# Two spectral and two attention layers on one core: constant matmuls and another order around the start of attention, another end of the layer

## The chip, the cores and the metric

The kernel runs on one core of a Trainium2 chip. A core has a matrix engine (TensorE, PE in the profile), a vector engine (VectorE, DVE), a scalar engine (ScalarE, ACT), a general one (GpSimd, POOL) and SyncE (SP), which only issues transfers. PE writes to PSUM, which the others read. The metric is the device time of one execution in microseconds (us); less is better. Before the change it is 1662.77 us, the median of three runs.

## The reference, cut to what matters

```python
def _layernorm(x):                       # over the last axis, eps 1e-5, no weights
    ...
def _A_ref(x, w_r, w_i):                 # spectral layer, x is 1 x 2048 x 512 bf16
    X = rfft2(x) * (w_r + 1j * w_i)
    return irfft2(X, s=(2048, 512)).astype(bf16)
def _B_ref(x, wq, wk, wv, wo):           # attention, 32 heads of 16, one k and one v for all heads
    q = (x @ wq).reshape(B, S, 32, 16).transpose(0, 2, 1, 3)
    k, v = x @ wk, x @ wv
    p = softmax(einsum("bhqd,bkd->bhqk", q, k) * 16 ** -0.5)
    o = einsum("bhqk,bkd->bhqd", p, v)
    return o.transpose(0, 2, 1, 3).reshape(B, S, 512) @ wo
x = x + A(layernorm(x));  x = x + B(layernorm(x))
x = x + A(layernorm(x));  x = x + B(layernorm(x))
```

## The kernel before

The 2048 tokens are split by their number modulo 4 into four blocks t, and each block into four tiles r of 128 tokens; `x_sb[:, r, t, :]` is the running sum and `xn_sb` its layernorm, both bf16 in SBUF. The layers run in the order A, B, A, B.

*Spectral layer* (`spectral_layer`). The transform over tokens begins with matmuls of `xn_sb` with tables (`over_s_sums`, L192), copied by ACT into `G` (`over_s_out`, L197); `over_s(3)` does the last block inside the layer, the blocks before it are done at the end of the attention layer ahead of it. Transforms over the other axis, the product with the weights and the way back follow. The end is `back_s(t)`: for each tile four matmuls (L391); even r add x by a matmul with the identity (L394) and are copied by ACT (L395), odd r are added by DVE (L397), and then `layernorm_group` takes the statistics of a pair of tiles (DVE, L125/L126), a square root (ACT, L128) and writes xn (L134 ACT, L136 POOL).

*What attention needs first* (`attention_inputs`). `block(t)` transposes xn into `xT` by eight and eight matmuls with the identity (L469), the first half copied by ACT (L472), the second by DVE (L474); four K matmuls (L478), copied into `KT` by ACT (L479); `kmax`, a maximum over KT by DVE (L480); 16 V matmuls (L485), whose result goes to `vaug` in four scaled copies, two by ACT (L490), two by DVE (L492). These share two PSUM banks ("mm"). `block(t - 1)` follows `back_s(t)`; `block(3)` comes last, and then `close`: an exponential of one column (L501), which makes ACT load its table, the bound of KT (L502, L503), and half of KT's rows rewritten (L505).

*Attention* (`attention_layer`) runs over 32 groups g (8 sets of 4 heads for each of 4 query blocks) in 514 steps n. A step has up to three score tiles of 128 keys by 512 queries for ACT (`act_step`: matmuls L583 into the three banks of `sc`, two such tiles in turn; one exponential L683 over all three) and one for DVE (`dve_step`: L583 into the bank `dv`, then L707 and L713, an exponential in integer arithmetic, whose error four scales of `vaug` even out). The matmuls with the values (`pv_step`, L695) come `LAG = 2` steps later and add up in one bank, `pv`. At the change of group the bank is copied by DVE (L598), its sums are inverted by way of DRAM, POOL normalises (L633, L639), and the queries of a later group are projected (L455 to L461). `chain()` fixes on each of PE, ACT, DVE and POOL the order in which the program was written.

*The layer's end* (L796 on). The output projection (`outproj`, L661) of tile k; `finish` adds x and stores to `x_sb`, either by ACT where a matmul with the identity has added x (L667), or by DVE (L669). `statistics` and `normal(t)` are the next layernorm (L756 to L776); `sequence(first)` does the `over_s_sums` of three units (one unit is a t and a quarter of the columns), `sequence_out` their copies to `G`. The last group's part is added to block four's tiles (k = 12 to 15) once POOL has normalised it (L633 `od`, then `woO` in L661). In the last layer `nxt` is None: no statistics, no sequences; `finish` also stores the output (L914).

Of the kernel before, what the change touches and what calls it, by code (L numbers as in the profile page):

```python
# [9 lines left out]
ACT = mybir.ActivationFunctionType  # L10
ALU = mybir.AluOpType
P = 128
# [6 lines left out]
NC = 4  # L19
# [77 lines left out]
def build_tables(nc, const):  # L97
# [5 lines left out]
    mhalf = const.tile([P, 1], F32, name="mhalf")  # L103
    nc.vector.memset(mhalf, -0.5)
    c["mhalf"] = mhalf
# [13 lines left out]
def layernorm_group(nc, lnpool, tabs, tiles):  # L119
# [3 lines left out]
    for i, (x_ap, _, _) in enumerate(tiles):  # L123
        stats = lnpool.tile([P, 6], F32, tag="ln_stats", bufs=4)
        nc.vector.bn_stats(stats, x_ap)  # L125
        nc.vector.bn_aggr(mv[:, i, :], stats)  # L126
# [74 lines left out]
def spectral_layer(nc, tc, tabs, shared, lnpool, x_sb, xn_sb, WT, WX, aw, nxt, loads):  # L201
# [5 lines left out]
    with (tc.tile_pool(name="workA", bufs=1) as work,  # L207
# [179 lines left out]
        def back_s(t):  # L387
            for r in range(R):
                ps = psum.tile([P, 512], F32, tag="pa")
                for k, (c, part) in enumerate(((0, 0), (0, 1), (1, 0), (1, 1))):  # L390
                    nc.tensor.matmul(ps, lhsT=IT[:, t, part, c, r * P:(r + 1) * P], rhs=U[:, t, part, c, :],  # L391
                                     start=(k == 0), stop=(k == 3 and r % 2 == 1))
                if r % 2 == 0:
                    nc.tensor.matmul(ps, lhsT=tabs["ident"], rhs=x_sb[:, r, t, :], start=False, stop=True)  # L394
                    nc.scalar.copy(out=x_sb[:, r, t, :], in_=ps)  # L395
                else:
                    v.tensor_tensor(out=x_sb[:, r, t, :], in0=ps, in1=x_sb[:, r, t, :], op=ALU.add)  # L397
                    layernorm_group(nc, lnpool, tabs, [(x_sb[:, q, t, :], xn_sb[:, q, t, :], (g, nc.scalar)[q % 2])
# [38 lines left out]
        prep["block"](T - 1, psum_b)  # L437
        prep["close"](xn_sb[:, R - 1, T - 1, 0:1])
# [3 lines left out]
def attention_inputs(nc, tabs, shared, xn_sb, aw):  # L442
# [21 lines left out]
    def block(t, psum):  # L464
        for half in range(2):
# [5 lines left out]
            if half == 0:  # L471
                nc.scalar.copy(out=dst, in_=ps)  # L472
            else:
# [6 lines left out]
        nc.vector.tensor_reduce(out=kmax[:, t:t + 1], in_=KT[:, ks], axis=mybir.AxisListType.X,  # L480
                                op=ALU.max, apply_absolute_value=True)
        psv = psum.tile([P, 4, DH], F32, tag="mm")
        for i in range(4):
            for c in range(NC):
                nc.tensor.matmul(psv[:, i, :], lhsT=xT[t][:, c, i, :], rhs=wv_sb[:, c, :],  # L485
                                 start=(c == 0), stop=(c == NC - 1))
        for j in range(4):
# [11 lines left out]
    def close(xn_last):  # L499
        dmyo = shared.tile([P, 1], F32, tag="dmyo", bufs=1)  # L500
        nc.scalar.activation(out=dmyo, in_=xn_last, func=ACT.Exp)  # L501
        nc.vector.tensor_reduce(out=kb[:, 0:1], in_=kmax, axis=mybir.AxisListType.X, op=ALU.max)  # L502
        nc.vector.tensor_scalar(out=kb[:, 1:2], in0=kb[:, 0:1], scalar1=tabs["KAB"][:, 1:2], scalar2=None, op0=ALU.mult)  # L503
        for a, b in ((0, 512), (512, S)):
            nc.vector.tensor_scalar(out=KT[:, a:b], in0=KT[:, a:b], scalar1=tabs["KAB"][:, 0:1], scalar2=kb[:, 1:2],  # L505
                                    op0=ALU.mult, op1=ALU.add)

# [469 lines left out]
```

## Time and profile before

| | us |
|---|---|
| runs | 1660.22, 1662.77, 1667.63 |
| median | 1662.77 |
| the profiled execution's own time | 1662.98 |
| its span, first to last instruction | 1661.2 |

| engine | busy us | share of the span | instructions |
|---|---|---|---|
| PE | 1404.5 | 85% | 12606 |
| DVE | 1549.5 | 93% | 2796 |
| ACT | 1506.4 | 91% | 1250 |
| POOL | 164.6 | 10% | 278 |

The mean granted TensorE clock is 0.971 of full speed. The page gives busy times, the span cut into 40 slices with the busy share of each in tenths, and the groups of instructions; a trace behind it answers for any stretch. A row of the timeline reads: start, duration, engine, line, operation, output <- inputs, partitions x elements and type, count, and in brackets the idle time before it with what ended it. For a matmul, 128*128 is rows * columns of the array, 32*128 a strip of 32 rows. PE's ends are modelled, so overlapping matmuls can show more busy time than they block.

### The profile page before, as it was taken

Reading aid. Unit: us, or ns where it says so; the run is one execution under the profiler, and the core shown is the slowest. Engines: PE = TensorE matmul, PEld = TensorE weight load, DVE = VectorE, ACT = ScalarE, POOL = GpSimd, SP = SyncE. Lnnn points to the kernel's source line nnn. Section 1 sums busy time; section 2 is a strip of 40 time slices with the busy share of each in tenths; the row PEclk is TensorE's granted clock in tenths of the full one; section 3 lists DMA queues with packets and bytes.
Section 4 is the critical chain, followed back from the end, with each engine's and each line's share of the span. In section 5 each row is a group of like instructions: output and inputs, shape, how many; then the busy total and the mean of one; then the engine's idle time right before and its main releaser. Section 6 shows DMA issues by size and latency. Waiting matters only on the chain.

```text
span 1661.2 us, 32022 instructions
## 1 busy us (share of the span) xinstructions
PE 1404.5 (85%) x12606; PEld 453.6 (27%) x12688; DVE 1549.5 (93%) x2796; ACT 1506.4 (91%) x1250; POOL 164.6 (10%) x278
## 2 busy tenths in 40 slices
PE   6778888888888888888888888888888888888887
PEld 3331222222222222222233222222222222222222
DVE  6977999999999999999778689999999999999996
ACT  5368999999999999999854689999999999999994
POOL 3210000000000000000112000000000000000002
PEclk9887999999999999999999689999999999999999
DMA  8000000000000010000020000000000000000002
GB/s 287 5 1 8 17 16 12 15 16 17 17 16 17 17 28 16 17 17 29 23 70 0 1 8 16 17 17 17 17 17 17 17 14 13 17 16 17 16 16 66
DMA packets 46535, 40.76 MB, mean 25 GB/s; under 512 B 30832, under 2 KB 34416, under 8 KB 46000
## 3 DMA queue, kind: packets, MB, share of 16 engines
q1 hardware_dynamic: 45712, 36.88, 7.6%
q8 instruction: 99, 1.62, 0.4%
q0 software_dynamic: 672, 1.84, 0.3%
q14 instruction: 52, 0.43, 0.1%
HBM read 33.57 MB, written 3.15 MB: 22 GB/s over the span
## 4 chain that ended last, share of the span: by engine, by line
DVE 39%; ACT 24%; PE 17%; issue 17%; DMA 1%; POOL 1%; DVEq 0%; SPq 0%; POOLq 0%; ACTq 0%
ACT e L683 23%; DVE t_new L707 15%; DVE s_new L713 12%; PE pv_new L695 6%; PE dv L583 3%; DVE o L598 2%; PE sc L583 2%; DVE qt L460 2%; PE fd L268 2%; DVE qt L461 2%; DVE stats L125 1%; PE ps L391 1%; PE ps L379 1%; DVE den L606 1%; PE ps L192 1%
## 5 line engine op out<-in xcount | busy, mean ns | idle before, releaser
L683 ACT ACTIVATE e<-sc 128x1536 bf16<-128x1536 f32 (+1 forms) x1028 | 1387.0, 1524 | 17.9 <-PE sc L583 17.5
L707 DVE TENSOR_SCALAR t_new<-dv 128x512 int16<-128x512 f32 x1016 | 693.9, 683 | 40.0 <-PE sc L583 21.1
L713 DVE TENSOR_SCALAR s_new<-t_new 128x2048 int16<-128x2048 int16 x1016 | 696.0, 686 | 0.0
L583 PE MATMUL dv<-qt,KT 32*128 32x512 bf16 x1016 | 389.9, 384 | 124.0 <-DVE t_new L707 116.3
L583 PE MATMUL sc<-qt,KT 32*128 32x512 bf16 x3080 | 423.7, 390 | 35.9 <-ACT e L683 3.2
L695 PE MATMUL pv_new<-s_new,vaug 128*32 128x512 bf16 x4064 | 413.3, 394 | 27.3 <-DVE qt L460 27.3
L695 PE MATMUL pv_new<-e,vaug 128*32 128x512 bf16 x3080 | 410.4, 387 | 0.4 <-ACT e L683 0.4
L583 PEld LDWEIGHTS <-KT 32*128 32x128 bf16 x4096 | 201.0, 91 | 731.2 <-issue 715.3
L695 PEld LDWEIGHTS <-vaug 128*32 128x32 bf16 x7144 | 135.7, 94 | 278.2 <-issue 264.7
L639 POOL TENSOR_TENSOR ot_new<-o,rb 128x176 bf16<-128x176 f32 (+1 forms) x96 | 56.4, 590 | 709.9 <-DVE s_new L713 653.1
L639 POOL TENSOR_TENSOR od<-o,rb 128x176 bf16<-128x176 f32 (+1 forms) x90 | 49.4, 549 | 597.5 <-DVE s_new L713 597.5
L455 PE MATMUL ps<-xT,wq_sb 128*128 128x512 bf16 x196 | 62.3, 378 | 13.9 <-DVE o L598 10.7
L379 PE MATMUL ps<-tab_PS,st 128*128 128x512 bf16 x126 | 34.1, 433 | 17.1 <-DVE st L327 13.9
L385 ACT CAST U<-ps 128x512 bf16<-128x512 f32 x24 | 14.1, 586 | 35.4 <-PE ps L379 35.4
L268 PE MATMUL fd<-X,tab_DT 128*128 128x512 bf16 x186 | 41.9, 379 | 3.1 <-DVE X L242 2.8
L460 DVE CAST qt<-ps 128x512 bf16<-128x512 f32 x64 | 44.2, 690 | 0.0
L598 DVE COPY o<-pv_new 128x512 f32<-128x512 f32 x64 | 43.8, 684 | 0.0
L274 ACT CAST xn_sb<-fd 128x512 bf16<-128x512 f32 x32 | 18.8, 586 | 26.9 <-PE fd L268 26.2
L125 DVE BATCH_NORM_STATS2 stats<-x_sb 128x6 f32<-128x512 bf16 x48 | 31.7, 676 | 7.1 <-ACT x_sb L395 3.7
L455 PEld LDWEIGHTS <-wq_sb 128*128 128x128 bf16 x256 | 24.5, 96 | 39.2 <-issue 15.2
L391 PE MATMUL ps<-U,IT 128*128 128x512 bf16 x122 | 32.2, 379 | 0.4
L192 PE MATMUL ps<-FT,xn_sb 128*128 128x512 bf16 x79 | 20.0, 406 | 14.4 <-ACT xn_sb L134 10.9
(134 smaller groups left out, 568.7 us busy)
## 6 DMA issues: line engine op xcount, KB each, us to landing
rb<-d SPq DMA_DIRECT2D x256, 64.0 KB
FT<-const_FT SPq DMA_DIRECT2D x8, 512.0 KB
IT<-const_IT SPq DMA_DIRECT2D x8, 512.0 KB
x_sb<-in_A_x_dram SPq DMA_DIRECT2D x4, 512.0 KB
ot_new<-od SPq DMA_DIRECT2D x120, 16.0 KB
out_dram<-x_sb POOLq DMA_DIRECT2D x14, 128.0 KB, 2.1
tab_DT<-const_DT SPq DMA_DIRECT2D x1, 1280.0 KB
wr_raw<-in_A_w_r_dram SPq DMA_DIRECT2D x1, 1028.0 KB
```

What stands on the lines that cost most here:

```text
L268: nc.tensor.matmul(pss[i], lhsT=DT[:, b, w, 128 * fb:128 * fb + 128], rhs=X[:, b, part, c, :, :].rearrange("p k j -> p (k j)"), start=star ...
L379: nc.tensor.matmul(ps, lhsT=st[c][:, t, vec, q, fb, :], rhs=PS[:, fb, w, :], start=(k == 0), stop=(k == 3))
L391: nc.tensor.matmul(ps, lhsT=IT[:, t, part, c, r * P:(r + 1) * P], rhs=U[:, t, part, c, :], start=(k == 0), stop=(k == 3 and r % 2 == 1))
L455: nc.tensor.matmul(ps, lhsT=wq_sb[:, c, hg, :], rhs=xTq[qb][:, c, :], start=(c == 0), stop=(c == NC - 1))
L460: nc.vector.tensor_copy(out=qt, in_=ps)
L583: nc.tensor.matmul(dst, lhsT=KT[hs, kc * P:(kc + 1) * P], rhs=QT[g][hs, :], start=True, stop=True)
L598: nc.vector.tensor_copy(out=o, in_=pv.pop(g))
L639: pace(nc.gpsimd.tensor_tensor(out=dst[:, a:b], in0=o[:, a:b], in1=rb[:, a:b], op=ALU.mult))
L683: nc.scalar.activation(out=e[:, 0:na, :], in_=sc[:, 0:na, :], func=ACT.Exp, scale=SCALE)
L695: nc.tensor.matmul(pv[g][32 * h:32 * h + 32, :], lhsT=vaug[:, max(j, 0), kc, :], rhs=rhs, start=(first_pv[(g, h)] == u), stop=(last_pv[(g, ...
L707: nc.vector.tensor_scalar(out=tb[(g, kc // 4)][:, kc % 4, :], in0=dv, scalar1=T_MUL, scalar2=T_ADD, op0=ALU.mult, op1=ALU.add)
L713: image[0] = nc.vector.tensor_scalar(out=s_new, in0=tb[(g, b)], scalar1=0.5, scalar2=16384.0 + PH_OFF[j], op0=ALU.mult, op1=ALU.add)
```

## The change

1. The constant `mhalf` goes; a 128 x 128 bf16 tile `zero` is set by POOL.
2. In `back_s`, the very last tile (r = 3, t = 3) adds x by the identity matmul and is copied by ACT, its statistics are read from PSUM, and the xn of r = 2 is written by DVE instead of POOL.
3. `block(t)` takes `kmax` from PSUM instead of from KT. In the built program it still stands behind the KT copy, and the bank is held until it is done.
4. `block(3)` gets 24 matmuls of 128*128x512 whose result (`idle`, in a bank of the other pool) is used by nothing: six with xn (in the built order one stands ahead of block 2's K matmuls and five behind its V matmuls), six with the first half of xT behind ACT's copy of it, ahead of K, and twelve with xT behind the V matmuls.
5. `close` is called inside `block(3)`, before the copies to `vaug`, and its one-column exponential reads xT instead of xn.
6. At step 1 of each attention layer six matmuls of `zero` with KT go into the bank of pv[0], which the first of them starts; group 0's matmuls then only add. At steps 2 to 5 two more each.
7. The layer's end: three of block four's tiles (all but the second) take x by the identity matmul and are finished by ACT. Their last part and `finish` come right behind the first sequence, ahead of `normal(2)`. The sequences are 3, 1, 3, 3 and 2 units long, the single ones in the banks of dv and pv, the copies to G bank by bank.

In all PE has 38 matmuls more in each attention layer with its lead-in.

```diff
-    mhalf = const.tile([P, 1], F32, name="mhalf")
-    nc.vector.memset(mhalf, -0.5)
-    c["mhalf"] = mhalf
+    zero = const.tile([P, P], BF, name="zero")
+    nc.gpsimd.memset(zero, 0.0)
+    c["zero"] = zero
...
-def layernorm_group(nc, lnpool, tabs, tiles):
+def layernorm_group(nc, lnpool, tabs, tiles, sums=None):
 
     n = len(tiles)
     mv = lnpool.tile([P, n, 2], F32, tag=f"ln_mv{n}", bufs=4)
     for i, (x_ap, _, _) in enumerate(tiles):
         stats = lnpool.tile([P, 6], F32, tag="ln_stats", bufs=4)
-        nc.vector.bn_stats(stats, x_ap)
+        nc.vector.bn_stats(stats, sums[i] if sums else x_ap)
         nc.vector.bn_aggr(mv[:, i, :], stats)
...
-                if r % 2 == 0:
-                    nc.tensor.matmul(ps, lhsT=tabs["ident"], rhs=x_sb[:, r, t, :], start=False, stop=True)
+                                     start=(k == 0), stop=(k == 3 and r % 2 == 1), skip_group_check=True)
+                if r % 2 == 0 or (r, t) == (R - 1, T - 1):
+                    nc.tensor.matmul(ps, lhsT=tabs["ident"], rhs=x_sb[:, r, t, :], start=False, stop=True,
+                                     skip_group_check=True)
                     nc.scalar.copy(out=x_sb[:, r, t, :], in_=ps)
                 else:
                     v.tensor_tensor(out=x_sb[:, r, t, :], in0=ps, in1=x_sb[:, r, t, :], op=ALU.add)
+                if (r, t) == (R - 1, T - 1):
+                    layernorm_group(nc, lnpool, tabs, [(x_sb[:, q, t, :], xn_sb[:, q, t, :], (v, nc.scalar)[q % 2])
+                                                       for q in (r - 1, r)], (x_sb[:, r - 1, t, :], ps))
+                elif r % 2 == 1:
                     layernorm_group(nc, lnpool, tabs, [(x_sb[:, q, t, :], xn_sb[:, q, t, :], (g, nc.scalar)[q % 2])
                                                        for q in (r - 1, r)])
 
...
-        prep["block"](T - 1, psum_b)
-        prep["close"](xn_sb[:, R - 1, T - 1, 0:1])
+        prep["block"](T - 1, psum_b, psum)
...
+    def filler(psum, rhs, n):
+
+        ps = psum.tile([P, 512], F32, tag="pa", name="idle")
+        for _ in range(n):
+            nc.tensor.matmul(ps, lhsT=tabs["ident"], rhs=rhs, start=True, stop=True)
+
+    def close(last):
+        dmyo = shared.tile([P, 1], F32, tag="dmyo", bufs=1)
+        nc.scalar.activation(out=dmyo, in_=last, func=ACT.Exp)
+        nc.vector.tensor_reduce(out=kb[:, 0:1], in_=kmax, axis=mybir.AxisListType.X, op=ALU.max)
+        nc.vector.tensor_scalar(out=kb[:, 1:2], in0=kb[:, 0:1], scalar1=tabs["KAB"][:, 1:2], scalar2=None, op0=ALU.mult)
+        for a, b in ((0, 512), (512, S)):
+            nc.vector.tensor_scalar(out=KT[:, a:b], in0=KT[:, a:b], scalar1=tabs["KAB"][:, 0:1], scalar2=kb[:, 1:2],
+                                    op0=ALU.mult, op1=ALU.add)
+
+    def block(t, psum, psum_idle=None):
+        if psum_idle is not None:
+            filler(psum_idle, xn_sb[:, 0, t, :], 6)
         for half in range(2):
             ps = psum.tile([P, 2, NC, P], BF, tag="mm")
             for i in range(2):
...
             dst = xT[t][:, :, 2 * half:2 * half + 2, :].rearrange("d c i p -> d i c p")
             if half == 0:
                 nc.scalar.copy(out=dst, in_=ps)
+                if psum_idle is not None:
+                    filler(psum_idle, xT[t][:, 0:2, 0:2, :], 6)
             else:
                 nc.vector.tensor_copy(out=dst, in_=ps)
         ks = slice(t * 512, (t + 1) * 512)
...
         for c in range(NC):
             nc.tensor.matmul(ps, lhsT=wka[:, c, :], rhs=xTq[t][:, c, :], start=(c == 0), stop=(c == NC - 1))
         nc.scalar.copy(out=KT[:, ks], in_=ps)
-        nc.vector.tensor_reduce(out=kmax[:, t:t + 1], in_=KT[:, ks], axis=mybir.AxisListType.X,
+        nc.vector.tensor_reduce(out=kmax[:, t:t + 1], in_=ps, axis=mybir.AxisListType.X,
                                 op=ALU.max, apply_absolute_value=True)
         psv = psum.tile([P, 4, DH], F32, tag="mm")
         for i in range(4):
             for c in range(NC):
                 nc.tensor.matmul(psv[:, i, :], lhsT=xT[t][:, c, i, :], rhs=wv_sb[:, c, :],
                                  start=(c == 0), stop=(c == NC - 1))
+        if psum_idle is not None:
+            filler(psum_idle, xTq[t][:, 0, :], 12)
+        if t == T - 1:
+            close(xT[t][:, NC - 1, 0:1, 0])
         for j in range(4):
             dst = vaug[:, j, 4 * t:4 * t + 4, 0:DH]
             if j % 2 == 0:
...
                 qproj(g, ps)
                 QT[g] = qevict(ps)
 
-    def close(xn_last):
-        dmyo = shared.tile([P, 1], F32, tag="dmyo", bufs=1)
-        nc.scalar.activation(out=dmyo, in_=xn_last, func=ACT.Exp)
-        nc.vector.tensor_reduce(out=kb[:, 0:1], in_=kmax, axis=mybir.AxisListType.X, op=ALU.max)
-        nc.vector.tensor_scalar(out=kb[:, 1:2], in0=kb[:, 0:1], scalar1=tabs["KAB"][:, 1:2], scalar2=None, op0=ALU.mult)
-        for a, b in ((0, 512), (512, S)):
-            nc.vector.tensor_scalar(out=KT[:, a:b], in0=KT[:, a:b], scalar1=tabs["KAB"][:, 0:1], scalar2=kb[:, 1:2],
-                                    op0=ALU.mult, op1=ALU.add)
-
-    return {"xT": xT, "KT": KT, "QT": QT, "qproj": qproj, "qevict": qevict, "block": block, "close": close}
+    return {"xT": xT, "KT": KT, "QT": QT, "qproj": qproj, "qevict": qevict, "block": block}
 
 
 def attention_layer(nc, tc, tabs, shared, lnpool, x_sb, xn_sb, aw, prep, nxt, store):
...
-                                 start=(first_pv[(g, h)] == u), stop=(last_pv[(g, h)] == u),
+                                 start=(g > 0 and first_pv[(g, h)] == u), stop=(last_pv[(g, h)] == u),
...
+            if n == 1:
+                pv_new = psp.tile([P, 512], F32, tag="pv")
+                pv[0] = pv_new
+                for i in range(6):
+                    nc.tensor.matmul(pv[0], lhsT=tabs["zero"], rhs=KT[:, 0:512], start=(i == 0), stop=False,
+                                     skip_group_check=True)
             if n in qproj_at:
                 ps = psp.tile([P, 512], F32, tag="pv")
                 qproj(qproj_at[n], ps)
                 later(1, lambda g=qproj_at[n], ps=ps: QT.__setitem__(g, qevict(ps)))
             else:
                 pv_step(n)
+            if LAG <= n < LAG + 4:
+                for _ in range(2):
+                    nc.tensor.matmul(pv[0], lhsT=tabs["zero"], rhs=KT[:, 0:512], start=False, stop=False,
+                                     skip_group_check=True)
...
-        def sequence(first):
+        def sequence(first, banks):
             if nxt is None:
                 return None
-            units = [divmod(u, 4) for u in range(first, first + 3)]
-            ps = psc.tile([P, 3, 512], F32, tag="sc", name="seq")
-            for i, (t, b) in enumerate(units):
-                over_s_sums(nc, nxt, xn_sb, t, b, ps[:, i, :])
-            return units, ps
+            units = [divmod(u, 4) for u in range(first, first + len(banks))]
+            for (t, b), ps in zip(units, banks):
+                over_s_sums(nc, nxt, xn_sb, t, b, ps)
+            return units, banks
 
         def sequence_out(arg):
             if nxt is None:
                 return
-            units, ps = arg
-            for i, (t, b) in enumerate(units):
-                over_s_out(nc, nxt, t, b, ps[:, i, :])
+            for (t, b), ps in zip(*arg):
+                over_s_out(nc, nxt, t, b, ps)
+
+        def three():
+            if nxt is None:
+                return []
+            ps = psc.tile([P, 3, 512], F32, tag="sc", name="three")
+            return [ps[:, i, :] for i in range(3)]
 
...
-        ps_a = psc.tile([P, 3, 512], F32, tag="sc", name="tri")
+        ps_a = psc.tile([P, 3, 512], F32, tag="sc", name="three")
+        pf = [ps_a[:, i, :] for i in range(3)]
         ps_b = psp.tile([P, 512], F32, tag="pv")
-        pf = [ps_a[:, 0, :], ps_a[:, 1, :], ps_a[:, 2, :], ps_b]
+        pf.append(ps_b)
         for i in range(4):
-            outproj(12 + i, pf[i], i % 2 == 0)
+            outproj(12 + i, pf[i], i != 1)
         rest()
-        statistics((9, 10, 11))
-        q0 = sequence(0)
+        statistics((9, 10))
+        q0 = sequence(0, three())
         sequence_out(q0)
-        rest = normal(2)
-        rest()
         for i in range(4):
             outproj(12 + i, pf[i], False, last_group=True)
         for i in range(4):
-            finish(12 + i, pf[i], i % 2 == 0)
-        q1 = sequence(3)
+            finish(12 + i, pf[i], i != 1)
+        ps_d = psd.tile([P, 512], F32, tag="dv", name="ps_d") if nxt is not None else None
+        q1 = sequence(3, [ps_d])
+        sequence_out(q1)
+        statistics((11,))
+        rest = normal(2)
+        q2 = sequence(4, three())
+        rest()
         statistics((12, 13, 14, 15))
-        sequence_out(q1)
+        sequence_out(q2)
+        q3 = sequence(7, three())
         rest = normal(3)
         rest()
-        for first in (6, 9):
-            q2 = sequence(first)
-            sequence_out(q2)
+        sequence_out(q3)
+        ps_e = psp.tile([P, 512], F32, tag="pv", name="ps_e") if nxt is not None else None
+        ps_f = psd.tile([P, 512], F32, tag="dv", name="ps_f") if nxt is not None else None
+        q4 = sequence(10, [ps_e, ps_f])
+        sequence_out(q4)
```

More of the change, by code (lines that the diff above doesn't have):

```diff
@@ L391, in back_s @@
                     nc.tensor.matmul(ps, lhsT=IT[:, t, part, c, r * P:(r + 1) * P], rhs=U[:, t, part, c, :],
-                                     start=(k == 0), stop=(k == 3 and r % 2 == 1))
-                if r % 2 == 0:
-                    nc.tensor.matmul(ps, lhsT=tabs["ident"], rhs=x_sb[:, r, t, :], start=False, stop=True)
+                                     start=(k == 0), stop=(k == 3 and r % 2 == 1), skip_group_check=True)
+                if r % 2 == 0 or (r, t) == (R - 1, T - 1):
+                    nc.tensor.matmul(ps, lhsT=tabs["ident"], rhs=x_sb[:, r, t, :], start=False, stop=True,
+                                     skip_group_check=True)
                     nc.scalar.copy(out=x_sb[:, r, t, :], in_=ps)
@@ L462, in qevict @@
         return qt
-    def block(t, psum):
+    def filler(psum, rhs, n):
[13 more added lines that the diff above has]
+            filler(psum_idle, xn_sb[:, 0, t, :], 6)
         for half in range(2):
```

## The prediction

> **What bounds the kernel now.** I read the page's head and slices first, then the busy time by stretches, then the start of each attention layer instruction by instruction. Times are us; the columns of a stretch are its length, the busy time and count of PE, PEld, DVE, ACT and POOL, the granted TensorE clock, the DMA share and GB/s.
>
> ```profile
> span 1661.2 us, 32022 instructions
> ...
> PEclk9887999999999999999999689999999999999999
> 200.00:700.00 500.00, 428.62 (x4157) 131.12 (x4176) 494.76 (x837) 500.00 (x372) 37.87 (x69) 1.00 0.06 17
> ```
>
> In the steady part of attention ACT never idles: 372 exponentials in 500 us, 1.344 us a step, with DVE at 99%. The change touches nothing there. What it can touch are the two dips of PEclk, at slices 3 and 4 and at slices 23 and 24, where attention begins.
>
> ```profile
> 118.50:158.45 39.95, 33.32 (x24) 0.63 0.00 1
> 939.50:978.94 39.44, 33.24 (x24) 0.65 0.00 1
> 117.40:147.50 30.10, 23.84 (x17) 0.50 0.00 1
> ```
>
> These are the exponentials of L683 alone (busy ACT, then clock, DMA share, GB/s). The first 24 steps of each layer take 39.95 and 39.44 us, where 24 x 1.344 = 32.3 would do. From 117.40 to 147.50 the clock is 0.50 from end to end, and in layer two the mean is as low, 0.65. The chain inside one such step:
>
> ```profile
> 130.04 0.60 PE L583 MATMUL dv<-qt,KT 32*128 32x512 bf16 x1
> ...
> 131.00 0.62 PE L695 MATMUL pv_new<-s_new,vaug 128*32 128x512 bf16 x4
> 131.18 1.45 ACT L683 ACTIVATE e<-sc 128x1536 bf16<-128x1536 f32 x1 [0.47 <-PE sc L583]
> ...
> 131.97 0.60 PE L583 MATMUL dv<-qt,KT 32*128 32x512 bf16 x1
> ```
>
> The next scores start 1.93 us after the last (130.04 to 131.97), and ACT idles 0.47 us for its scores each time. So PE at half clock sets the pace here, and nowhere else in attention.
>
> Why the clock falls shows in the stretches between its changes. In layer one it falls at 113.77 and rises at 147.90, ten times 3.413 us later; in layer two it falls at 929.55. Cut backwards from the falls in pieces of that length, the last windows at full clock are the first four rows, and the low stretch (PE alone) is the fifth:
>
> ```profile
> 103.53:106.94 3.41, 2.07 (x21) 1.28 (x19) 3.25 (x12) 3.12 (x7) 0.97 (x2) 1.00 0.00 0
> 106.94:110.35 3.41, 2.03 (x28) 1.31 (x28) 1.58 (x6) 2.35 (x6) 0.90 (x2) 1.00 0.00 0
> 110.35:113.77 3.42, 1.17 (x10) 0.77 (x12) 1.02 (x3) 1.90 (x4) 0.00 (x0) 1.00 0.00 0
> 926.14:929.55 3.41, 1.48 (x21) 0.88 (x21) 1.70 (x7) 2.31 (x5) 1.53 (x2) 1.00 0.00 0
> 113.77:147.90 34.13, 30.88 (x175) 0.50 0.00 1
> ```
>
> The clock held after windows with 2.07 and 2.03 us of PE work and fell after 1.17 and 1.48. Then it did not rise through ten windows in which PE was 90% busy. So busy time alone isn't what lifts it: the work of those windows is narrow (32 rows or 32 columns of the array, the 32*128 and 128*32 above), and where it did rise, PE ran full 128*128 matmuls (the stretches again of PE alone, the last two rows of matmuls one by one):
>
> ```profile
> 885.18:888.59 3.41, 3.41 (x10) 0.50 0.00 0
> 888.59:892.00 3.41, 3.41 (x18) 1.00 0.00 0
> ...
> 884.60 4.30 PE L379 MATMUL ps<-tab_PS,st 128*128 128x512 bf16 x10
> 843.84 5.34 PE L192 MATMUL seq<-FT,xn_sb 128*128 128x512 bf16 x24 [1.27 <-ACT x_sb L667]
> ```
>
> One window of full matmuls, 4.30 / 10 = 0.43 us each at half clock, and the next stands at 1.00; at full clock one costs 5.34 / 24 = 0.22.
>
> **The change part by part.** Per layer it adds 24 full matmuls ahead of the first score (6 with xn, 6 after ACT's xT copy, 12 after the V matmuls) and 14 zero matmuls into pv[0] (6 at step 1, 2 at each of steps 2 to 5), changes two orders and rebuilds the layer's end. Here is the lead-in of layer one that the 24 are laid into, and its counterpart in layer two:
>
> ```profile
> 109.04 0.57 ACT L479 CAST KT<-ps 128x512 bf16<-128x512 f32 x1
> 109.64 0.69 DVE L480 TENSOR_REDUCE kmax<-KT 128x1 f32<-128x512 bf16 x1 [1.35 <-ACT KT L479]
> 109.75 1.28 ACT L501 ACT_TABLE_LOAD   x1
> ...
> 111.25 1.00 ACT L472 COPY xT<-ps 128x1024 bf16<-128x1024 bf16 x1
> 111.76 0.61 PE L469 MATMUL ps<-tab_ident,xn_sb 128*128 128x128 bf16 x8 [1.50 <-DVE vaug L492]
> 113.15 1.32 PE L478 MATMUL ps<-xT,wka 128*128 128x512 bf16 x3 [0.79 <-DVE xT L474]
> 116.38 0.99 DVE L505 TENSOR_SCALAR KT<-KT,tab_KAB,kb 128x512 bf16<-128x512 bf16 x2
> 117.43 0.60 PE L583 MATMUL dv<-qt,KT 32*128 32x512 bf16 x1 [2.54 <-DVE KT L505]
> 118.51 10.18 ACT L683 ACTIVATE e<-sc 128x1536 bf16<-128x1536 f32 x7 [2.31 <-PE sc L583]
> ...
> 929.07 0.57 ACT L479 CAST KT<-ps 128x512 bf16<-128x512 f32 x1
> 938.43 0.60 PE L583 MATMUL dv<-qt,KT 32*128 32x512 bf16 x1 [2.54 <-DVE KT L505]
> ```
>
> *The clock.* With six more full matmuls (1.3 us) the windows ending near 110 and 929.5 come to about 3.3 and 2.8 us; the next holds six more and the K matmuls, the next the twelve, and the one over the first scores the zeros. All lie above the 2.03 that held. If the clock holds to the first steps, these run at 1.344 from the start: 39.95 - 32.3 = 7.6 and 39.44 - 32.3 = 7.1. I leave 0.8 of each standing, since two steps at the first change of group remain long even after the clock is back (exponentials 1.90 apart):
>
> ```profile
> 153.87 1.45 ACT L683 ACTIVATE e<-sc 128x1536 bf16<-128x1536 f32 x1 [0.39 <-PE sc L583]
> 155.77 5.48 ACT L683 ACTIVATE e<-sc 128x1536 bf16<-128x1536 f32 x4 [0.45 <-PE sc L583]
> ```
>
> Gain 6.8 + 6.3 = 13.1; bounds: 14.7 if nothing stays, and 11.5 if 1.6 of each stays. The first score to first exponential, 1.08 at half clock (117.43 to 118.51), halves in its matmul part: -0.45 a layer, -0.9.
>
> [...]
>
> *The lead-in.* From the KT copy of block 2 to the first score it takes 8.4 in layer one and 9.4 in layer two, whose clock fell earlier. kmax now reads PSUM, but comes behind the KT copy still, and its bank comes free only after the reduce: block 3's transposes wait for kmax (end 110.33) instead of for the copy (109.61), +0.6. Against that the table load (1.28) leaves the path of ACT's xT copy, which ran 111.25 to 112.25 behind it; now it can follow the transposes at 110.8. The second eight are then done near 111.5, not 112.37; the six fillers behind ACT's xT copy (111.8) stand ahead of K on PE: 6 x 0.22 = 1.3, to 113.1, where K started at 113.15. K ends at 114.2; the table load at 113.1 is out of the way of the KT copy; kmax, kb and KT follow as before to 117.2. The twelve, 2.6 from 114.8, end at 117.4, beside that DVE chain. So layer one: 0 (+1 if a semaphore comes late on each side, -0.3 if K's own 0.3 at half clock is gained), taken as +0.2; layer two: the same 8.4 instead of 9.4, -0.8. Together -0.6. Were the cover of DVE's chain gone, the twelve would cost their 2.6.
>
> *The zeros.* The six at step 1 (1.3) lie where pv has not begun; two a step add 0.43 to a step in which PE's weight loads show a gap of this size at full clock:
>
> ```profile
> 156.12 0.09 PEld L583 LDWEIGHTS <-KT 32*128 32x128 bf16 x1 [0.42 <-issue]
> ```
>
> Four such gaps of 0.42 take 4 x 0.43 almost whole: 0 to +0.8 a layer, nearer 0; +0.4 for both.
>
> *The spectral layer's end.* The last tile through an ident matmul and an ACT copy, xn by DVE and kmax in another place swap pieces of 0.4 to 0.8 between ACT, DVE and POOL: 0, bounds -0.5 and +0.5 a layer.
>
> *The layer's end* (once, at 835 to 853; the last layer has no spectral work behind it):
>
> ```profile
> 841.83 0.56 ACT L667 CAST x_sb<-tri 128x512 bf16<-128x512 f32 x1
> ...
> 847.75 1.52 ACT L773 ACTIVATE xn_sb<-x_sb,nb,rstd 128x512 bf16<-128x512 bf16 x2 [0.50 <-DVE nb L768]
> 849.17 3.00 ACT L197 CAST G<-seq 128x512 bf16<-128x512 f32 x6
> 852.22 1.02 PE L192 MATMUL ps<-FT,xn_sb 128*128 128x512 bf16 x4 [3.05 <-ACT G L197]
> ```
>
> The finishing copies move ahead of normal(2), so up from 841.83 by about its two ACT passes, 1.5 to 2. But normal(2) and the statistics of tile 11, which stood in front, now stand between them and the last xn passes (847.75 to 849.27): these come at the same time or up to 0.4 later. What is won is at the end: over_s(3) waits for three copies of G (half of the 3.00) from 849.6 instead of six from 849.17, so starts at 851.2 to 851.5 instead of 852.22. -0.75, between -1.2 (the xn passes not later) and +0.3 (two of the single banks waiting a copy each of 0.5).
>
> *The tail.*
>
> ```profile
> 1656.72 0.68 DVE L669 TENSOR_TENSOR x_sb<-ps_b,x_sb 128x512 bf16<-128x512 f32 x1
> 1656.90 0.59 ACT L667 CAST x_sb<-tri 128x512 bf16<-128x512 f32 x1 [0.81 <-DVE x_sb L669]
> ```
>
> The last tile moves from DVE to behind ACT's: done at 1658.1 instead of 1657.40. Its store follows, the other stores overlap: +0.3, between 0 and +0.7.
>
> *Sum.* The profiled run took 1662.98 (span 1661.2 and 1.8 around it), the median is 1662.77; they are one level. 1662.98 - 13.1 - 0.9 - 0.6 + 0.4 + 0 - 0.75 + 0.3 = 1648.3. With all terms at one bound it is 1643.5 or 1655; 1644.5 to 1652 unless they all go one way.
>
> **The rivals.** (a) *The clock falls all the same in the first steps*, because zeros don't count or two a step are too few. The clock held above 2.03 us of work, but steady attention holds it too with 428.62 of 500; against: the start differs from steady work by its first two steps without pv, which the six zeros fill. If so, 13.1 and 0.9 are lost and the 14 zeros at 0.43 lie on PE's path: of 6 us a layer in all, half in steps whose pv work is short: 0 to +3 a layer; 1661 to 1667, say 1663.
>
> (b) *One layer of two, or half of each.* The window's phase is free, and layer two's last K window had 1.48. Where the clock falls before the fillers, twelve in a row at 0.43 (5.2) fill one window and lift it, as ten did at 884.60; the fillers then cost 2 to 3 on the lead-in. 1662.98 less half of 14 plus 0 to 2: 1655 to 1658.
>
> (c) *Slower: the added work runs at half clock throughout.* If 24 fillers don't keep it up, the six ahead of K (2.6 instead of 1.3) push K and all behind it by 1.3; the twelve, 5.2 from 116.2, end at 121.4, 2.7 after KT is ready (117.4 + 1.3); the zeros add 14 x 0.43 = 6 on the PE that sets the pace there. Up to 10 a layer, 1683; it decides once the first score finds the clock at 0.50. Against it: 16 full matmuls (12 added, 4 of K) within the two windows from 108; one window of them lifted the clock at 885.18.
>
> (d) *The layer's end loses.* With q1 and q4 in banks of dv and pv there is more waiting between copies and matmuls; six copies of G take 3.00, so no more than that: +3 on the forecast, 1651.
>
> **How the numbers follow.** The clock held, with or without (d): 0.72 ((d) 0.06 of it). (b): 0.11. (a): 0.09. (c): 0.08. One layer's gain alone, 7, is near 0.5% (8.3 us, about the least that a measurement of this kernel tells from no change). So faster: 0.72 and a small part of (b), 0.74; same: most of (b) and (a), 0.18; slower: (c), 0.08. The likeliest one's range is 1644.5 to 1652; reaching through (b) to the lower end of (a), so as to leave out no more than two in ten, 1643.5 to 1661. Predicted: 1648.3.
>
> **What would show it.** PEclk at 9 in slices 3 and 23; 1.00 in each stretch from 110 to 150 and its counterpart; the first 24 exponentials of a layer within 33 to 34 us; first score 8.4 after block 2's KT copy in both layers; over_s(3)'s matmuls behind the third copy of G, some 0.7 earlier after the last od; the last ACT copy behind the last but one. Wrong if the clock shows 0.50 after the first score for more than one window, if K waits for fillers beyond 113.2, or if ACT still idles for sc at step 10.

## The result, and the profile after

The changed kernel took 1649.27 us, median of five runs (1648.27 to 1655.24), against 1662.77 before (the three runs above and two more, 1660.22 to 1667.63): ratio 0.9921, 95% interval 0.9894 to 0.9948. That is 13.5 us less; 1648.3 was predicted, with 1643.5 to 1661 as the range.

The profiled one of the five is the slowest. From its page:

```profile
span 1653.4 us, 32260 instructions
PEclk9899999999999999999998999999999999999999
```

The dips at slices 3 and 4 and at 23 and 24 are gone; the 8 of slice 2 stands in both kernels, that of slice 22 lies in the spectral layer. What the row can't show, since its 9 stands for 90% or more, is why this execution is slow: a finer cut shows 0.95, not 1.00, nearly everywhere in it; its mean is 0.943, that of the four others 0.992 or 0.993 at spans of 1646.5 to 1647.9. So that a clock of 1.00 is compared with a clock of 1.00, the rows of after come from a second profile of the unchanged changed kernel, run e1 below (1646.76, span 1645.0). The exponentials alone, first 24 steps of each layer (length, busy ACT, clock, DMA share, GB/s):

```profile
117.70:150.44 32.74, 31.92 (x24) 1.00 0.01 2
927.84:960.72 32.88, 32.04 (x24) 1.00 0.01 2
```

39.95 and 39.44 us have become 32.74 and 32.88, where the steady pace would give 32.3, at 1.00 instead of 0.63 and 0.65. The 0.95 execution does nearly the same (32.94 and 33.08); what it loses is elsewhere, the largest part, 3.85 of the 8.4 us by which its span is longer than e1's, between over_s(3) and block 2's KT copy (80.45 us, e1 76.60).

The lead-in of layer one in e1, by the timeline:

```profile
108.74 0.56 ACT L502 CAST KT<-ps 128x512 bf16<-128x512 f32 x1
109.33 0.69 DVE L503 TENSOR_REDUCE kmax<-ps 128x1 f32<-128x512 f32 x1 [0.96 <-ACT KT L502]
110.72 1.01 ACT L493 COPY xT<-ps 128x1024 bf16<-128x1024 bf16 x1 [0.31 <-PE ps L490]
111.75 1.28 ACT L476 ACT_TABLE_LOAD   x1
111.79 1.46 PE L472 MATMUL idle<-xT,tab_ident 128*128 128x512 bf16 x6 [0.44 <-ACT xT L493]
113.08 1.03 PE L501 MATMUL ps<-xT,wka 128*128 128x512 bf16 x3
114.35 2.75 PE L472 MATMUL idle<-xT,tab_ident 128*128 128x512 bf16 x12
116.01 0.99 DVE L480 TENSOR_SCALAR KT<-KT,tab_KAB,kb 128x512 bf16<-128x512 bf16 x2
117.07 0.39 PE L601 MATMUL dv<-qt,KT 32*128 32x512 bf16 x1
117.72 1.45 ACT L701 ACTIVATE e<-sc 128x1536 bf16<-128x1536 f32 x1 [1.88 <-PE sc L601]
```

It reads as it was worked out: xT's copy no longer behind the table load, six constant matmuls in front of K at 0.22 each, K where it was, the twelve (114.35 to 117.10) ending with the DVE chain (117.00), beside it and not behind it.

The stages of both profiles, from the start of one instruction to the start of the next (us; each is a difference of two starts in the trace):

| stage | before | after (e1) | difference |
|---|---|---|---|
| start to KT copy of block 2 | 109.04 | 108.74 | -0.30 |
| KT copy to first score, layer one | 8.39 | 8.33 | -0.06 |
| first score to first exponential | 1.08 | 0.65 | -0.43 |
| 24 steps | 39.94 | 32.72 | -7.22 |
| step 24 to 488 | 625.11 | 625.07 | -0.04 |
| step 488 to the last `od` | 51.23 | 50.71 | -0.52 |
| `od` to over_s(3) | 17.43 | 16.05 | -1.38 |
| over_s(3) to KT copy of block 2 | 76.85 | 76.60 | -0.25 |
| KT copy to first score, layer two | 9.36 | 8.33 | -1.03 |
| first score to first exponential | 1.08 | 0.65 | -0.43 |
| 24 steps | 39.43 | 32.87 | -6.56 |
| step 24 to 488 | 625.10 | 626.23 | +1.13 |
| step 488 to the last `od` | 49.23 | 49.81 | +0.58 |
| `od` to the end | 7.94 | 8.22 | +0.28 |

The differences add up to -16.2, the difference of the spans (1661.2 and 1645.0). That is more than the 13.5 between the medians: e1's profile is of the fastest of its five executions.

The largest loss, step 24 to 488 of layer two, wasn't forecast. 1.2 us more than before stand there in the profiles of every version with the new orders (e5 and e7 to e12 below) and in none of those without them (e2, e3, e4, e6); in e1 eight steps lose 0.12 to 0.25 us each, most of them 64 steps apart. So the orders cost it, whatever the constants and the layer's end do. Why isn't settled.

The layer's end in e1, timeline:

```profile
826.23 1.27 POOL L651 TENSOR_TENSOR od<-o,rb 128x512 bf16<-128x512 f32 x1 [2.77 <-DMA rb<-d]
831.25 0.60 ACT L685 CAST x_sb<-three 128x512 bf16<-128x512 f32 x1
839.26 1.52 ACT L801 ACTIVATE xn_sb<-x_sb,nb,rstd 128x512 bf16<-128x512 bf16 x2 [0.50 <-DVE nb L796]
840.69 1.54 ACT L197 CAST G<-three 128x512 bf16<-128x512 f32 x3
842.28 3.61 PE L192 MATMUL ps<-FT,xn_sb 128*128 128x512 bf16 x16 [2.91 <-ACT G L197]
```

Counted from `od`, the last xn passes start at 13.03 (before: 847.75 - 834.79 = 12.96), the copies of G at 14.46 (before 14.38), and over_s(3) behind the third copy at 16.05 instead of behind the sixth at 17.43.

### The profile page after: what moved, and what is told of

The parts are those of the page before. It is cut to its first block, busy times and chain, and to the rows that moved or that the text cites. A ratio compares the mean times of both kernels' runs of the same rounds, so it can differ in the third digit from the quotient of the medians.

```text
span 1653.4 us, 32260 instructions
## 1 busy us (share of the span) xinstructions
PE 1428.4 (86%) x12768; PEld 461.3 (28%) x12768; DVE 1551.4 (94%) x2793; ACT 1509.0 (91%) x1254; POOL 163.2 (10%) x277
## 4 chain that ended last, share of the span: by engine, by line
ACT 32%; DVE 29%; issue 21%; PE 16%; POOL 1%; DMA 1%; SPq 0%; DVEq 0%; POOLq 0%; ACTq 0%
ACT e L701 31%; DVE t_new L725 11%; DVE s_new L731 9%; PE pv_new L713 4%; PE fd L268 2%; PE dv L601 2%; DVE o L616 2%; DVE qt L464 2%; PE sc L601 2%; DVE qt L465 1%; DVE stats L125 1%; PE tri L679 1%; PE ps L391 1%; PE ps L379 1%; PE ps L192 1%
## 5 line engine op out<-in xcount | busy, mean ns | idle before, releaser
L601 PE MATMUL dv<-qt,KT 32*128 32x512 bf16 x1016 | 384.1, 378 | 108.1 <-DVE t_new L725 106.0
L601 PE MATMUL sc<-qt,KT 32*128 32x512 bf16 x3080 | 409.0, 383 | 33.9 <-ACT e L701 4.3
L459 PE MATMUL ps<-xT,wq_sb 128*128 128x512 bf16 x256 | 67.3, 387 | 11.4 <-DVE o L616 11.4
L379 PE MATMUL ps<-tab_PS,st 128*128 128x512 bf16 x128 | 36.1, 448 | 16.2 <-DVE st L327 12.7
```

The costliest lines, as they stand in the source:

```text
L379: nc.tensor.matmul(ps, lhsT=st[c][:, t, vec, q, fb, :], rhs=PS[:, fb, w, :], start=(k == 0), stop=(k == 3))
L459: nc.tensor.matmul(ps, lhsT=wq_sb[:, c, hg, :], rhs=xTq[qb][:, c, :], start=(c == 0), stop=(c == NC - 1))
L601: nc.tensor.matmul(dst, lhsT=KT[hs, kc * P:(kc + 1) * P], rhs=QT[g][hs, :], start=True, stop=True)
```

## The experiments

All times are medians against runs of the kernel before in the same job (one set of runs on one chip); their medians lay at 1664 to 1666. The ratio on record isn't the quotient of the two medians (e1: 1648.31 / 1664.99 = 0.9900); gains are read from it, with its interval. "Full" matmuls are 128*128 by 512 columns.

**e1: the change again.**

> The changed kernel once more, since the profiled run of it stood at a granted clock of 0.95 from end to end (span 1653.4) while its four other runs have a mean of 0.992 and spans of 1646.5 to 1647.9. Theory (clock gained at the start of attention): median 1648 to 1650; a profile at 1.00 shows the first 24 exponentials of each layer in 32.5 to 33.5 us (39.95 and 39.44 before), first score 8.4 us after block 2's KT copy. Rival (the gain has another source): these 24 steps still take over 36 us.

Measured: 1648.31 (1646.76 to 1653.21), ratio 0.9913 (0.9898 to 0.9929). The rows above are its profile; the theory's numbers hold, the rival's don't.

**e2, e3, e4: the constants alone, and each kind alone.** To the kernel before:

```diff
+        filler(psum_idle, ...)            # e2, e3: 6 with xn, 6 after ACT's xT copy, 12 after V
...
+            if n == 1: six matmuls of zero into pv[0]          # e2, e4
+            if LAG <= n < LAG + 4: two more                    # e2, e4
```

> Before, with the 24 constant matmuls ahead of the first score and the 14 zero matmuls of each layer, every order and the layer's end as before. Theory (clock): 1649 to 1651, 12 to 14 us less than before, PEclk 1.00 from block 3 on in both attention layers. Rival (the new orders and the layer's end bring most): less than 5 us gained.

> Before, with the 24 constant matmuls alone. Theory (the zeros carry the clock over the first two steps, which have no pv): the clock is 1.00 at the first score and falls within two windows, 7 us; nearly nothing gained, 1660 to 1664. Rival (once up, the steps' own work holds it): 1649 to 1651, as with the zeros.

> Before, with the 14 zero matmuls of each layer alone; the first score finds the clock at 0.50. Theory (full matmuls lift the clock where narrow ones don't): the six at step 1, 2.6 us at half clock, and the two a step fill one window, the clock rises near 125 and 946 instead of 147.9 and 967.1: 1654 to 1658. Rival (14 in this spread are too few): the clock stays at 0.50 to 148 and the zeros cost up to 3 us a layer, 1664 to 1669.

Measured: e2 1651.98, ratio 0.9931 (0.9917 to 0.9945); e3 1659.23, 0.9970 (0.9958 to 0.9982); e4 1657.84, 0.9969 (0.9953 to 0.9984). Both kinds together bring 0.69% of e1's 0.87%, either alone 0.30 or 0.31. e2 lies 1 us above what was expected, and its profile isn't at 1.00 all through: the clock falls for one window in layer one, 145.36 to 148.77, at the first change of group, and those 24 steps take 33.87. e3 gained more than the "nearly nothing" of its theory. Windows of 3.413 us of e3, in layer one and layer two (columns as in the prediction: length, PE, PEld, DVE, ACT, POOL, clock, DMA share, GB/s):

```profile
116.08:119.50 3.42, 2.85 (x18) 1.03 (x17) 2.61 (x8) 0.98 (x2) 0.00 (x0) 1.00 0.00 0
119.50:122.91 3.41, 2.37 (x19) 0.68 (x15) 2.07 (x3) 3.41 (x4) 0.00 (x0) 1.00 0.00 0
122.91:126.32 3.41, 3.41 (x18) 0.70 (x16) 2.72 (x5) 3.41 (x3) 0.00 (x0) 0.50 0.00 0
...
945.52:948.94 3.42, 2.87 (x22) 0.88 (x21) 3.33 (x7) 3.42 (x4) 0.00 (x0) 1.00 0.00 0
948.94:952.35 3.41, 3.41 (x23) 0.54 (x22) 2.38 (x4) 3.41 (x3) 0.00 (x0) 0.50 0.02 5
```

The 24 matmuls carry the clock to the first scores; then it falls after a window with 2.37 us of PE work in layer one, 2.87 in layer two, all of it narrow. Windows of e4:

```profile
116.87:120.28 3.41, 2.38 (x10) 0.37 (x11) 2.00 (x4) 1.65 (x2) 0.00 (x0) 0.50 0.00 0
120.28:123.70 3.42, 3.42 (x13) 0.82 (x11) 0.52 (x1) 1.22 (x2) 0.00 (x0) 0.50 0.00 0
123.70:127.11 3.41, 3.26 (x22) 0.75 (x20) 1.72 (x4) 3.41 (x3) 0.00 (x0) 1.00 0.00 0
```

Here the clock is 0.50 at the first score, and the window at 120.28, which holds most of the six zeros, lifts it, 24 us earlier than in the kernel before. The theory of e4 (1654 to 1658) is met by the median and in the profile (1654.29); but of its twelve runs five lie at 1662 to 1664, at mean clocks of 0.978 to 0.981 (the profiled one: 0.986). None of these was profiled; probably the lift came later in them.

**e5, e12, e6: what is not constants.** e5 and e12 are the change without `filler` calls and zeros; e6 is the kernel before with the new layer's end.

> The change without its constant matmuls (24 and 14 a layer left out): the new orders and the layer's end alone. Theory (they are worth little beside the clock): the clock falls at the start of attention as before, the layer's end gains 1.4 as measured from the last od to over_s(3), the tail loses 0.3, and K starts up to 1 us earlier without the six matmuls ahead of it: 1 to 4 us less than before. Rival (constants and orders hang together, the gap of 3.7 us between e2 and e1 is all theirs): 4 us or more less than before.

> e5 once more, since its six runs spread from 1656.5 (mean clock 0.977) to 1667.6 (0.968) and only the slowest was profiled. Theory (orders and layer's end gain 2 to 3 us, the rest of its 6 us is the clock, which comes back at another window by the phase of the run): over both jobs the time goes with the mean clock, the runs at 0.970 to 0.972 lie 2 to 4 us under runs of before at the same clock. Rival (the orders themselves lift the clock earlier): its mean clock is above that of before in nearly all runs, and the profile shows 0.50 ending before 140 and 960.

> Before, with the new layer's end alone. Theory: 1.5 us less from the last od to over_s(3), 0.3 more in the tail, 1.2 less in all, which five rounds can hardly tell from nothing. Rival (the layer's end loses in banks of dv and pv): slower than before.

Measured: e5 1658.93, 0.9959 (0.9946 to 0.9972); e12 1659.06, 0.9962 (0.9947 to 0.9977); e6 1665.03, 0.9998 (0.9988 to 1.0008). So orders and layer's end without constants bring 6 to 7 us, not the 1 to 4 that was expected; on top of the constants (e1 against e2) they bring 0.18%, 3 us. Part of it is plain in e12's profile: `od` to over_s(3) 15.55 (17.43 before), KT copy to first score 8.24 and 8.09 (8.39 and 9.36), together 3.3, less 0.3 in the tail and 1.2 in layer two's steps. The rest goes with the clock. The runs of e12 stand at a mean clock of 0.972 to 0.977, the 63 runs of before in these jobs at 0.966 to 0.974. At equal clock there is still a gain: the three runs of e5 and e12 at 0.971 and 0.972 took 1660.7 to 1661.0, those of before at these clocks 1663.2 and 1662.6 in the mean. Windows of e12 in layer two:

```profile
954.65:958.06 3.41, 3.41 (x21) 0.64 (x20) 2.17 (x4) 2.75 (x2) 0.00 (x0) 0.50 0.00 0
958.06:961.47 3.41, 3.39 (x36) 0.87 (x33) 2.18 (x4) 3.13 (x4) 0.00 (x0) 1.00 0.00 0
```

It rises at 958, 22 us behind the first exponential (936.34), where the profile of before needed 27.6 (939.51 to 967.1); the 24 steps take 37.04 instead of 39.43. The rival of e12 (the orders lift the clock earlier) isn't shown by this. In layer one of the same profile the clock rises at 145.69, not before 140; in the profile of e5, its slowest run, it rises at 148.59 and 971.20, as late as before; and in that of e6, with the old orders, at 140.65 and 956.43. The point of the rise differs by the execution, and why the runs of e5 and e12 stand at a higher mean clock stays open: nothing in the orders adds work to these steps. e6 alone can't be told from nothing; its profile has 15.68 from `od` to over_s(3), 1.75 less, but the gain of 1.2 that was expected lies within its interval of +-1.7 us.

**e9: transposes instead of constant matmuls.** The zeros stay:

```diff
-            nc.tensor.matmul(ps, lhsT=tabs["ident"], rhs=rhs, start=True, stop=True)
+            for c in range(4):
+                nc.tensor.transpose(ps[:, c, :], rhs[c], tabs["ident"])
```

> The change with each of the 24 constant matmuls ahead of the first score replaced by four transposes of 128x128 with the same identity (what the kernel computes stays; the zeros stay too). Theory (any work of the full array counts): the clock holds to the first score as in e1, 1648 to 1651. [...]

Measured: 1649.46 (1647.59 to 1653.58), 0.9916 (0.9901 to 0.9930), as the change. A window of e9 ahead of layer two, and the PE work in it from its timeline:

```profile
920.17:923.58 3.41, 2.93 (x50) 2.50 (x47) 1.74 (x4) 2.32 (x5) 0.00 (x0) 1.00 0.02 5
```

```profile
920.11 1.33 PE L473 MATMUL idle<-tab_ident,xn_sb 128*128 128x128 bf16 x21
921.40 1.27 PE L491 MATMUL ps<-tab_ident,xn_sb 128*128 128x128 bf16 x16
923.12 0.68 PE L473 MATMUL idle<-tab_ident,xT 128*128 128x128 bf16 x9 [0.44 <-ACT xT L494]
```

But for four V matmuls of 16 columns that end in its first 0.1 us, PE does nothing but transposes in this window, and the clock is 1.00 in it, in the next, and at the first score. In layer one it is 1.00 in each window from 107.80 to 121.45, with 2.93 to 3.37 us of PE work. Here the transposes of `nc.tensor.transpose`, which the profile lists as MATMUL, held it as well as the matmuls in their place did (e1: 1.00 in each window from 109.81 to 126.88, with 2.84 to 3.41 us).

**e11: six zeros.** `if LAG <= n < LAG + 4: ...` left out of the change.

> The change with the six zero matmuls at step 1 alone; the two at each of steps 2 to 5 are left out. In e3, without any, the clock fell after a window of 6 pv and 9 scores in layer one and after 10 and 12 in layer two. Theory (those windows are the ones at risk, and the six cover only the first): the clock falls within 12 us of the first score in some layers, median 2 to 6 us above e1. Rival (the six are enough): 1647 to 1650, and the first 24 steps 0.5 to 1 us shorter, as PE has less to do in them.

Measured: 1649.40 (1645.49 to 1655.66), 0.9916 (0.9897 to 0.9936). In its profile the clock stays at 1.00 through the first twelve steps of both layers: the theory, a fall within 12 us of the first score, didn't come true. The 24 steps of layer two take 32.68 (32.87 with the eight), those of layer one 33.68, with a fall of one window at 144.42, at the first change of group, where e2 and e8 fell too with the eight in place. So the rival fits the time and the clock, but 0.19 is less than the 0.5 to 1 us that it gave. The wider spread leaves open whether the eight protect against something in other executions.

**e7, e8, e10: the clock held elsewhere too.** To the change:

```diff
+            for _ in range(10):           # e7, e8, e10: behind q4 = sequence(10, ...)
+                nc.tensor.matmul(ps_i, lhsT=tabs["ident"], rhs=xn_sb[:, 0, 2, :], start=True, stop=True)
...
+                    if t == 0 and part == 1:
+                        idle(8)           # e8, e10: in back_d, behind its first tile
+        idle(28 if loads else 6)          # e8, e10: ahead of back_d(0)
...
+            if s0[1] - 1 <= n < s0[1] + LAG: two zero matmuls into pv[0]     # e10
```

> The change, with ten more constant matmuls behind the last sequence of the layer's end, where PE waits 2.9 us for ACT's copies of G ahead of over_s(3). Theory (in many executions the clock falls there, as in the profiles of e2 to e4, where the 16 matmuls of over_s(3) took 6.5 us instead of 3.6): its median falls by 1 to 3 us against the change alone, and the profile shows over_s(3) at 1.00. Rival (DVE sets the pace behind it anyway, or the ten delay over_s(3)): 0 to +1.

> As e7, and constant matmuls in the two spectral layers also ahead of the way back (28 in layer one, 6 in layer three) and behind its first tile of each half (8 each). Theory: the clock falls in no window of the spectral layers but the one near 55 to 62, another 0.5 to 2 us less than e7 and a smaller spread. Rival (PE is off the path there, DVE and ACT set it): as e7, or up to 1 us more where the matmuls stand before work that is ready.

> e8 with two more zero matmuls into pv[0] at each of the steps 17, 18 and 19, where group 0 runs out and a window holds 4 pv and 12 score matmuls. In profiles e2, e7 and e8 the clock fell there and the first 24 steps took 1.2 to 2 us more; in e1 a window of the same count held. Theory: no fall there in any execution, median 0.5 to 2 us under e8, mean clock 0.998 or more. Rival (the steps are bound by ACT and the six cost what they save): as e8, 1646 to 1648.

Why there: over_s(3) in e3's timeline takes nearly twice the 3.61 of e1.

```profile
850.82 6.54 PE L192 MATMUL ps<-FT,xn_sb 128*128 128x512 bf16 x16 [3.04 <-ACT G L197]
```

Measured: e7 1650.09, 0.9908 (0.9895 to 0.9921); e8 1646.99 (1646.34 to 1649.25), 0.9894 (0.9881 to 0.9906); e10 1647.80 (1647.33 to 1648.58), 0.9905 (0.9892 to 0.9918). The mean clock is 0.991 to 0.993 in e7, 0.997 or 0.998 in e8, 0.997 to 0.999 in e10. e7's profile has 15.93 from `od` to over_s(3), but 79.58 from there to block 2's KT copy (76.60 in e1): the clock falls further on, at 872 and at 886, and nothing is won: the theory of e7 (1 to 3 us less) missed. e8 closes these gaps too and has 76.62. Its profile still falls once, in layer one:

```profile
140.49:143.91 3.42, 2.48 (x23) 0.87 (x17) 2.81 (x5) 3.36 (x4) 0.00 (x0) 1.00 0.02 5
143.91:147.32 3.41, 2.62 (x15) 0.80 (x19) 2.62 (x6) 2.42 (x3) 0.00 (x0) 0.50 0.04 7
```

and e1 held through a window of almost the same work:

```profile
140.53:143.95 3.42, 2.58 (x23) 0.87 (x17) 2.81 (x6) 3.36 (x4) 0.00 (x0) 1.00 0.00 0
```

e10 removes this fall, but the 24 steps take 33.26 and 33.41, 0.54 more than in e1 in each layer, and the fall cost 2 us only where it came: the rival. So the clock can be held at 0.997 to 0.999 in the mean (e10's profile falls for one window near the end of each attention layer, at 792.88 and 1605.25), and the spread shrinks from 6.5 us (e1) to 1.3 (e10), but the median isn't lower by more than the intervals allow. e8 is the lowest of all versions, by 1.3 us against e1, with overlapping intervals and in another job.

## Why the prediction was right, point by point

*The clock as the source*: shown. e2 gains by constants alone, and e3 and e4, in whose first steps the clock falls back to 0.50 or starts there, gain less; -7.22 and -6.56 in the first 24 steps stand against the 6.8 and 6.3 of the sum. The 0.8 per layer that was left standing was a little too much: 32.72 and 32.87 against 32.3 leave 0.4 and 0.6, the zeros' cost included.

*First score to first exponential*: -0.43 each, -0.45 in the sum.

*The lead-in*: -0.06 and -1.03 measured, +0.2 and -0.8 in the sum. Every step of it is in the rows of e1, the second layer's 8.33 equal to the first's.

*The zeros' cost*: +0.4 for both layers in the sum. e11 without eight of the fourteen is 0.19 faster in the steps of layer two, which lies within the 0 to 0.8 a layer; in layer one a fall of the clock hides the comparison, and the six weren't tested alone.

*The spectral layer's end*: 0, with bounds of 0.5; -0.30 and -0.25 measured, which also hold what the clock did there.

*The layer's end* was the mis-sized term: -0.75, between -1.2 and +0.3, and it measured -1.38, beyond the bound. The sum let the copies of G start 0.43 later (849.6 for 849.17), on the reason that the last xn passes "come at the same time or up to 0.4 later"; they came 0.07 later and the copies 0.08, so nearly the whole of three copies of G (1.5) was won. For passes that are not later at all, 3.00 / 2 = 1.5 is already more than the bound of -1.2. e5, e6 and e12 show the same stage at 15.55 to 15.79.

*The tail*: +0.28 in the profile, +0.3 in the sum.

*One reason was wrong though the result was right.* The prediction took 2.03 us of PE work in a window as enough to hold the clock, since that had held. e3's clock fell after 2.37 in layer one and after 2.87 in layer two, where PE was 84% busy. So the gap that PE has in the first two steps is not all that the zeros make up for: the work of these steps is narrow. With full-array work about as many microseconds held the clock (e9's transposes, 2.93 at 920.17), and e4's window with most of the six zeros lifted it (120.28); the last section has a count by area. The sum came out because the zeros stood in the windows of the first steps.

*What the prediction didn't see*: that the clock moves elsewhere too, by the run. Its sum has no term for the up to 6.5 us by which one execution of e1 differs from another; the profiles show falls at over_s(3), between the halves of `back_d`, at the first change of group and near the end of an attention layer. Nor has it one for the 1.1 us that the orders cost in layer two's steps; in e1's profile the clock, the lead-in and the two ends each gained more than forecast, which outweighs it. Of the rivals, e3 is what (a) looks like (the clock falls in the first steps) and e4 what (b) looks like (it falls ahead of them and is lifted), but neither came up in the two profiles of the change. The phase that (b) calls free does differ: before, the clock falls 4.73 us behind block 2's KT copy in layer one (113.77 and 109.04) and 0.48 behind it in layer two (929.55 and 929.07). (c), half clock throughout, came up in no profile; (d), a loss at the layer's end, is ruled out by the -1.38.

## What to carry to other kernels

Look at the granted clock by stretches before counting instructions: two stretches of 34 and 38 us at 0.50, in a kernel at 0.971 in the mean, made up most of a gain of 0.8%, and 38 useless full-array operations a layer, most of them laid into waits that were there anyway, bought it back. Here they had to cover the wait and also the first steps of the narrow work behind it: e2 with both gained 0.69%, e3 and e4 with one of them 0.30 and 0.31%. Where the remaining falls differed from run to run, holding the clock there (e8, e10, four and five runs) narrowed the spread (2.9 and 1.3 us, e1 6.5) more than it moved the median (1646.99 and 1647.80, e1 1648.31).

## What the runs showed of the hardware that wasn't expected

The time of an execution goes with its mean clock, with the same program: among the 63 runs of before in these jobs the twenty at 0.969 took 1665.6 in the mean, the nine at 0.972 1662.6, the three at 0.974 1659.9.

Narrow work kept the clock up in the steady part of before (200 to 700 at 1.00, PE 429 of 500 us) and did not lift it through ten windows at 90% busy (113.77 to 147.90 at 0.50). Busy time doesn't tell such windows apart: at full clock it fell behind one that was 84% busy (e3, 945.52) and held through one that was about 40% busy (e1, 884.64 to 888.05, where PE idles until 886.69 and then runs 25 full matmuls in 5.79 us).

A count by area goes further, though not all the way, in the profiles of before and after. The full stretches between two changes of clock there are whole multiples of 3.413 us (3.413, 6.827, 10.240 and 34.133 at 0.50; 30.719, 40.960 and 44.373 among those at the full clock, 1.00 or, in after, 0.95), so both are cut at the changes into windows of that length. Count a full matmul of 512 columns as 1, one of fewer columns as its share, a narrow one as a quarter (32 of 128 rows or columns), one across a border by the part inside. The 36 windows with 0.50 behind them count 0 to 5.8, the 925 with the full clock behind them 4.7 or more, whatever it was in the window itself. The ranges overlap: before, 5.7 at 62.57 had 0.50 behind it and 4.9 at 144.49 the full clock. The ten windows fit: between 200 and 697 in the profile of before no window counts less than 6.3, while the narrow steps from 120.6 to 147.9, which start 1.93 us apart (130.04, 131.97) and not 1.344, count 3.9 to 5.0. That the clock goes by this count isn't shown: the quarter is taken from the shape, and some matmuls can be missing from a trace, so the figures are rough.

Which windows lift the clock isn't settled: the kernel before was lifted at 147.90 in one profile, e12 at 145.69 and e6 near 140, with the same instructions in those steps.

One execution of the change and one of e2 ran at a mean of 0.943, the profiled one at 0.95 in nearly every stretch and not at 1.00: a third level. The profiled one took 5.6 to 7.0 us more than the other executions of the change (1655.24 against 1648.27 to 1649.67). Against e1's profile its span is 8.4 longer, of which 3.85 lie behind over_s(3), where its clock fell to 0.50 as it did in others; the 4.5 that are left are an upper estimate of what the level itself cost.
